# A two-part state-space kernel: one small load moved between DMA queues, two products moved to VectorE, half-block stores at the end, and a new hand-written order

## The chip, the cores and the metric

The kernel runs on one core of a Trainium2 chip. A core has five engines with a queue each: TensorE (PE in the profile, its weight loads PEld), VectorE (DVE), ScalarE (ACT), GpSimd (POOL) and SyncE (SP), and 16 DMA engines that carry the transfers which SP and ACT issue. The metric is the device time of one execution in microseconds, the median of several runs. Lower is better.

## What is computed

Two independent sequence operators over 2048 steps and 640 channels, their outputs laid side by side in one (1, 2048, 1280) bfloat16 result.

```python
# A: a diagonal complex recurrence between two dense products
Lam_bar = jnp.exp(jnp.exp(log_dt) * Lam)
B_bar = ((Lam_bar - 1.0) / Lam)[:, None] * (B_re + 1j * B_im)
Bu = jnp.einsum("bld,pd->blp", x + 0j, B_bar)
for t in range(L):
    h = Lam_bar[None, :] * h + Bu[:, t, :]
y = 2.0 * jnp.einsum("blp,dp->bld", hseq, Cmat).real + x * Dskip
# B: a 4-tap filter on k, a product with v, a long convolution by FFT, a gate
k_shift = sum of four shifted copies of k, each times a tap of shift_k
kv = k_shift * v
y = irfft(rfft(kv) * rfft(ssm_k))[:S] + kv * ssm_D
out_b = q * y
```

## The kernel before

**Part A.** The 2048 steps are split into four phases q (step modulo 4), the 640 states into five blocks j of 128. `z{q}{j}` is the input product of phase q and block j on PE, ten matmuls of 128x512 (two parts, real and imaginary, by five pieces of the contraction), evicted by ACT to the tile F (`ze{q}{j}`, line 764). The phases are made in the order 1, 2, 3, 0, and each has to have the previous phase's sum, turned by the state's eigenvalue, added to it. That addition is either four more matmuls with the diagonal matrices diagL (lines 437 and 438) or, for the pairs (q, j) in the set `BYDVE`, five DVE operations after the eviction (`zd{q}{j}`, `dve_odd`, lines 464 to 468). Before, `BYDVE` holds (2, 0), (2, 1) and (2, 2). Then a scan over phase 0 runs on DVE (`rs{j}`, line 453), `h0{j}` turns it back, `h1{j}` to `h3{j}` spread it to the other phases (`dve_odd` again), and `p{i}{q}` on PE multiplies a block of 128 rows of phase q by the output matrix (20 matmuls of 128x320, line 478). Three quarters of the later blocks get x times Dskip added on DVE while they leave PSUM (`yo{i}{q}`, line 508, from `xd{i}`, line 504); the rest get it by three small matmuls per half (line 485) and leave by ACT (line 489). `yd{i}{q}` stores them.

**Part B.** It goes over five groups G of 128 channels: transposing loads of k and v (`kT`, `vT`), a copy of k with its two halves of partitions swapped (`kS`), the four taps as 32 small matmuls in two halves (`tap{G}_{m}`, line 553), the product with v on DVE straight from PSUM (`kv{G}_{m}`, line 558), a store of it to memory (`kvo`) and a reload in another layout (`kvs`). The long convolution is a transform in two steps on PE (`s1h`, `s2h` for the filter, `s1k`, `s2k` for kv, lines 576 and 590 to 593), a complex product on DVE in two halves (`y{G}_{hf}`, lines 603 to 606), the way back (`inv`, lines 614 to 617), a transposing DMA (`zt`), a last small product (`fin`, line 635), the gate with q on DVE (`ob`, line 640) and a store (`od`). For each group, ACT makes all evictions between these steps (`s1he`, `s2he`, `s1ke`, `s2ke`, `zs`). The set `KVA` names groups whose taps ACT evicts into the tile kT (`kve`), so that DVE multiplies once over the whole group in SBUF; before, it is empty.

**The start.** Small rows (log_dt, the two Lambda rows, Dskip, the taps) are loaded on ACT's queue. SP loads B, block by block (B0, B1, then x1 in two pieces, then B2 to B4, x2 and so on). PE runs eight matmuls on zeros (`wm0`, `wm1`), transposes the small rows (`vt`) and the blocks of B (`bt0` to `bt7`, line 389), whose evictions go to ACT (line 395) and DVE (line 397). From the small rows come, through exp, rho, rr, Fi, trig1, lam on ACT and DVE, the eigenvalue and its powers (`pow`, on POOL). `G0` to `G3` are sine and cosine tables for the transforms (ACT, lines 373, 153, 154); POOL prepares their phases (`gp`) and those of the scan's tables (`tp`). `dcol` loads a column of ssm_D in two strided DMAs (line 515, on ACT's queue), which `had{G}` (line 537) adds to the filter.

**What sets the order.** There is no loop left in the program text that orders the work: every step is an item of a plan (`make_plan`) with an engine, an assumed cost and its dependencies, and `ORDER` is a written list of all of them, with the PSUM slot behind an `@`. Each engine and each DMA queue gets its items in that order and works through them without overtaking. A PSUM slot is free again when the item that evicts it is done. DMAs use a fixed number of completion slots in turn, so an issue can also wait for an older DMA of the same slot. The costs in the plan serve only the search that made the list.

## Time and profile before

| | us |
|---|---|
| median of 3 runs | 202.76 (202.07 to 203.42) |
| the profiled execution | 203.54 |
| its span, first to last instruction | 201.8 |
| PE busy | 191.2 |
| DVE busy | 169.2 |
| ACT busy | 146.6 |
| POOL busy | 31.4 |

The profile of one execution gives a page (busy time, the span in 40 slices, groups of instructions by line) and a trace that can be asked for timelines and for busy time by stretch. In a timeline the columns are start, duration (of the merged run), engine, line, operation, output and inputs, count, and in brackets how long the engine sat idle before it and what ended that. PEclk or "granted clock" is the share of full TensorE speed that was granted. A group's line ends with its busy total, the mean duration of one in ns, and the idle time just before.

### The profile page before, as it was taken

To read this page: it belongs to the slowest core of one execution; us is meant where nothing else is said; L and a number is where in the kernel's file an instruction comes from. 1 tells how busy PE (TensorE), PEld (TensorE's weight loads), DVE (VectorE), ACT (ScalarE), POOL (GpSimd) and SP (SyncE) were. 2 spreads that over 40 slices of the span, in tenths; PEclk is the share of its full clock that TensorE was granted. 3 is DMA by queue.
4 is the path that set the end of the run, shared out by engine and by line. 5 is a ranking of instruction groups with operands and counts; after the bars stand their busy time and mean duration, and the time that the engine had idled before them with its cause. 6 is when DMAs were issued, how large, how long until landed. Compare 5 with 4: busy or idle time off the path is not lost.

```text
span 201.8 us, 5456 instructions
## 1 busy us (share of the span) xinstructions
PE 191.2 (95%) x2294; PEld 135.1 (67%) x2303; DVE 169.2 (84%) x279; ACT 146.6 (73%) x178; POOL 31.4 (16%) x68
## 2 busy tenths in 40 slices
PE   7848999999999999999999999999999999899992
PEld 2525444444444875488878897689977998787771
DVE  2822578999989999999999999999999999985561
ACT  2268769979985987899978899689977799350010
POOL 7881898900000000000000000000000000000000
PEclk9995899999999999999999999999999999999999
DMA  5999999749968999998999899799839569739944
GB/s 142 223 235 204 181 202 233 127 132 227 195 127 236 198 158 257 178 190 131 169 241 207 180 190 184 182 258 184 178 97 142 143 137 187 131 79 192 209 145 131
DMA packets 110667, 36.01 MB, mean 178 GB/s; under 512 B 104877, under 2 KB 109618, under 8 KB 110642
## 3 DMA queue, kind: packets, MB, share of 16 engines
q1 hardware_dynamic: 110544, 35.64, 91.7%
q8 instruction: 18, 0.29, 0.7%
q14 instruction: 7, 0.06, 0.1%
q10 hardware_dynamic: 98, 0.02, 0.1%
HBM read 10.66 MB, written 7.86 MB: 92 GB/s over the span
## 4 chain that ended last, share of the span: by engine, by line
PE 89%; DMA 3%; POOL 3%; ACT 2%; issue 1%; DVE 1%; ACTq 0%; DVEq 0%; POOLq 0%
PE ps L478 20%; PE ps L434 20%; PE ps L576 6%; PE ps L553 5%; PE ps L590 5%; PE ps L592 4%; PE ps L591 4%; PE ps L593 4%; DMA zz<-zz 3%; PE ps L438 3%; PE ps L635 3%; PE ps L437 2%; PE ps L614 2%; PE ps L616 2%; PE ps L615 2%; PE ps L617 2%
## 5 line engine op out<-in xcount | busy, mean ns | idle before, releaser
L434 PE MATMUL ps<-xT,BT 128*128 128x512 bf16 x187 | 47.3, 390 | 0.6 <-issue 0.4
L478 PE MATMUL ps<-Cs,F 128*128 128x320 bf16 x320 | 46.9, 300 | 0.0
L478 PEld LDWEIGHTS <-F 128*128 128x128 bf16 x320 | 29.9, 98 | 11.0
L434 PEld LDWEIGHTS <-BT 128*128 128x128 bf16 x192 | 18.6, 100 | 23.0 <-issue 3.1
L580 ACT CAST As_h<-ps 128x1024 bf16<-128x1024 f32 x20 | 20.3, 1022 | 7.9 <-PE ps L576 7.9
L764 ACT CAST F<-ps 128x1024 bf16<-128x1024 f32 x20 | 20.1, 1007 | 5.1 <-PE ps L434 3.2
L622 ACT CAST zz<-ps 128x1024 bf16<-128x1024 f32 x20 | 19.2, 1039 | 5.7 <-PE ps L617 5.5
L580 ACT CAST As_kv<-ps 128x1024 bf16<-128x1024 f32 x20 | 20.0, 1035 | 2.7 <-PE ps L576 2.7
L596 ACT CAST Xs<-ps 128x1024 bf16<-128x1024 f32 x20 | 19.9, 1052 | 0.6 <-PE ps L593 0.6
L596 ACT CAST Hf<-ps 128x1024 bf16<-128x1024 f32 x20 | 19.8, 1072 | 0.5 <-PE ps L593 0.5
L590 PE MATMUL ps<-As_kv,Gre 128*128 128x128 bf16 x80 | 17.6, 220 | 0.0
L590 PE MATMUL ps<-As_h,Gre 128*128 128x128 bf16 x80 | 17.6, 220 | 0.0
L614 PE MATMUL ps<-Xs,Hre 128*128 128x128 bf16 x80 | 17.6, 220 | 0.0
L592 PE MATMUL ps<-As_h,Gim 128*128 128x128 bf16 x80 | 17.6, 220 | 0.0
L592 PE MATMUL ps<-As_kv,Gim 128*128 128x128 bf16 x80 | 17.6, 220 | 0.0
L616 PE MATMUL ps<-Xs,Him 128*128 128x128 bf16 x80 | 17.6, 219 | 0.0
L591 PE MATMUL ps<-As_h,nGim 128*128 128x128 bf16 x80 | 17.5, 219 | 0.0
L615 PE MATMUL ps<-Xs,nHim 128*128 128x128 bf16 x80 | 17.5, 219 | 0.0
L593 PE MATMUL ps<-As_h,Gre 128*128 128x128 bf16 x80 | 17.5, 219 | 0.0
L591 PE MATMUL ps<-As_kv,nGim 128*128 128x128 bf16 x80 | 17.5, 219 | 0.0
L593 PE MATMUL ps<-As_kv,Gre 128*128 128x128 bf16 x80 | 17.5, 219 | 0.0
L617 PE MATMUL ps<-Xs,Hre 128*128 128x128 bf16 x80 | 17.5, 219 | 0.0
(163 smaller groups left out, 454.7 us busy)
## 6 DMA issues: line engine op xcount, KB each, us to landing
h_st<-in_B_ssm_k_dram SPq DMA_DIRECT2D x10, 256.0 KB, 4.7
kv_rows<-vT SPq DMA_DIRECT2D x5, 512.0 KB, 5.1
kv_st<-kv_rows SPq DMA_DIRECT2D x10, 256.0 KB, 4.1
qb<-in_B_q_dram SPq DMA_DIRECT2D x5, 512.0 KB, 4.8
out_dram<-yo SPq DMA_DIRECT2D x16, 160.0 KB, 3.6
out_dram<-qb SPq DMA_DIRECT2D x5, 512.0 KB, 6.5
kS<-kT SPq DMA_DIRECT2D x10, 129.0 KB, 2.5
BT<-in_A_x_dram SPq DMA_DIRECT2D x3, 320.0 KB, 5.2
```

The source lines that it names most:

```text
L434: mm(ps[:, r, :], lhsT=self.BT[:, r, k, j * 128:(j + 1) * 128], rhs=xT[:, k, :], start=(k == 0), stop=(prev is None and k == NT - 1))
L478: mm(ps[:, b, 0:320], lhsT=self.F(p, j)[:, r, ts], rhs=self.Cs[:, r, j, c0:c0 + 320], start=(j == 0 and r == 0), stop=((i, p // 2) in SKD ...
L580: self.nc.scalar.copy(out=As[:].rearrange("p k (h s) -> p h k s", h=2)[:, :, :, 16 * q:16 * q + 16], in_=ps[:].rearrange("p h (k s) -> p h ...
L590: mm(o_re, lhsT=self.Gre[:, k1, :], rhs=re, start=True, stop=False)
L591: mm(o_re, lhsT=self.nGim[:, k1, :], rhs=im, start=False, stop=True)
L592: mm(o_im, lhsT=self.Gim[:, k1, :], rhs=re, start=True, stop=False)
L593: mm(o_im, lhsT=self.Gre[:, k1, :], rhs=im, start=False, stop=True)
L596: self.nc.scalar.copy(out=dst[:, :, o:o + 128 * n], in_=ps[:] if n == 4 else ps.rearrange("p (r n) -> p r n", r=2))
L614: mm(o_re, lhsT=self.Hre[:, k1, :], rhs=yre, start=True, stop=False)
L615: mm(o_re, lhsT=self.nHim[:, k1, :], rhs=yim, start=False, stop=True)
L616: mm(o_im, lhsT=self.Him[:, k1, :], rhs=yre, start=True, stop=False)
L617: mm(o_im, lhsT=self.Hre[:, k1, :], rhs=yim, start=False, stop=True)
```

## The change

- The load of the ssm_D column (`dcol`) is issued on SP's queue, after x2, instead of on ACT's.
- `BYDVE` also holds (2, 3) and (2, 4): phase 2 of all five blocks gets its sum on DVE instead of by matmuls.
- `KVA` holds groups 1 and 2: ACT evicts their taps, DVE multiplies once in SBUF. The next load of kT then waits for that product.
- The last output block, (3, 3), is made, added to and stored in two halves of 320 columns.
- Some assumed costs in the plan are other (pow 6.0 instead of 4.2, gam 3.4 instead of 2.4, the latency of the B loads), some ACT steps are bound behind the loads on ACT's queue, and `ORDER` is a new list throughout, with other PSUM slots.
- `act_ha` and `dve_ha` are new functions that nothing calls, since the set `HA` is empty.

```diff
-BYDVE = {(2, j) for j in range(3)}
-KVA = set()
+BYDVE = {(2, j) for j in range(5)}
+KVA = {1, 2}
...
+HA = set()
+LAST = {(3, 3)}
...
-    def pe_proj(self, i, p, ps):
+    def pe_proj(self, i, p, ps, bs=(0, 1)):
         mm = self.nc.tensor.matmul
+        self.part["p", i, p] = ps
...
-        for b in range(2):
+        for b in bs:
...
+    def dve_yoh(self, y, i, q, b):
+        c = slice(320 * b, 320 * b + 320)
+        self.nc.vector.tensor_tensor(out=self.__dict__[f"yo{y}"][:, q % 2, c], in0=self.part["p", i, q][:, b, 0:320],
+                                     in1=self.xd[:, i % 2, q % 2, c], op=ALU.add)
+
+    def store_yoh(self, y, i, q, b):
+        c = slice(320 * b, 320 * b + 320)
+        self.nc.sync.dma_start(out=self.o2[512 * i:512 * i + 512, c].rearrange("(m p) d -> p m d", p=4)[q],
+                               in_=self.__dict__[f"yo{y}"][:, q % 2, c])
...
-            self.nc.scalar.dma_start(out=self.dcol_b[64 * h:64 * h + 64:16, :, 0:61], in_=src)
+            self.nc.sync.dma_start(out=self.dcol_b[64 * h:64 * h + 64:16, :, 0:61], in_=src)
...
-    dma("dcol", "ACT", 1.0, 0.0, ["~l_sk", "pc"], lambda: K.load_dcol(), lat=2.4)
+    dma("dcol", "SP", 1.1, 0.3, ["~x2", "pc"], lambda: K.load_dcol())
...
-    A("exp", "ACT", 0.3, ["vc"], lambda: K.act_exp())
+    A("exp", "ACT", 0.3, ["vc", "~l_sk"], lambda: K.act_exp())
...
+            if (i, q) in LAST and sk:
+                hd = [f"h{q}{j}" for j in range(NT)] + cs_all
+                A(f"p{i}{q}a", "PE", 10 * P320, hd, lambda ps, i=i, q=q: K.pe_proj(i, q, ps, (0,)), take=f"p{i}{q}", group=f"P{x}")
+                A(f"yo{i}{q}a", "DVE", 0.42, [f"p{i}{q}a", f"xd{i}"] + old, lambda y=y, q=q, i=i: K.dve_yoh(y % 2, i, q, 0), group=f"P{x}")
+                dma(f"yd{i}{q}a", "SP", 0.45, 0.4, [f"yo{i}{q}a"], lambda y=y, i=i, q=q: K.store_yoh(y % 2, i, q, 0), group=f"P{x}")
...
```

The first steps of both lists, engine by engine (items in the order in which the engine gets them):

```
ACT before: l_ldt l_lim l_lre l_dsk l_sk exp btf0 bte1 dcol rr G3 ze10 bte3 bte4 ze11 trig1 tab0 ze12 aRM bte5 ze13 ze21 ze20 G2
ACT after:  l_ldt l_lim l_lre l_dsk l_sk btf0 exp rr bte1 G2 trig1 bte3 ze10 ze11 bte4 tab0 ze12 bte5 G3 ze21 aRM ze20 ze22 tab1
PE before:  wm0 wm1 vt bt0 bt2 bt1 skt z10a z11a z10 bt3 z11 bt6 bt4 bt5 z12 bt7 z13 z21 z20 z14 z22 tap0_0 tap0_1 z30
PE after:   wm0 bt0 vt wm1 bt1 skt bt2 z10a z10 bt3 z11a bt6 z11 bt4 bt5 z12 z21 bt7 z20 z22 z13 tap0_1 tap0_0 z24 z23 z31 z14 z30 z01
DVE before: dc zer vc dc2 bte0 bte2 rho Fi skc bte6 rden bte7 dS0 lam dD dRM dL zd20 zd21 kv0_0 dS1 zd22 kv0_1 cs0 cs1 had0 rs0
DVE after:  dc vc bte0 rho Fi bte2 skc zer dc2 bte6 rden dD lam dL bte7 dS0 zd21 dRM zd20 kv0_1 dS1 zd22 kv0_0 cs1 nG cs0 zd23 cs3 cs2 had0 zd24 rs1
SP before:  B0 B1 x1a x1 B2 B3 B4 x2 kT0 vT0 x3 kS0 CT0 x0 CT1 hs0 kvo0 kT1 vT1
SP after:   B0 B1 x1a x1 B2 B3 B4 x2 dcol kT0 x3 kS0 vT0 CT0 CT1 kT1 x0 kS1 hs0 kvo0
```

The last steps of the new list on PE are inv4 (four parts), p12, p13, p22, fin4_1, p23, the first half of p33, fin4_0, p32, the second half of p33; on SP the last are the stores of the first half of (3, 3), of (2, 3), of group 4's output (od_4), of (3, 2) and of the second half of (3, 3).

## The prediction

> **What bounds the kernel now.** I read the page's busy table and its 40 slices, then busy time by stretch, then the timelines of the first 25 us and of the end, then the groups by line.

> ```profile
> PE 191.2 (95%) x2294; PEld 135.1 (67%) x2303; DVE 169.2 (84%) x279; ACT 146.6 (73%) x178; POOL 31.4 (16%) x68
> ...
> DVE  2822578999989999999999999999999999985561
> ...
> PEclk9995899999999999999999999999999999999999
> ```
> ```profile
> 15.90:21.90 6.00, 5.76 (x29) 3.48 (x30) 1.13 (x4) 4.34 (x8) 1.37 (x2) 0.51 1.14 174
> ...
> 57.60:100.00 42.40, 42.14 (x579) 28.96 (x576) 40.57 (x59) 35.93 (x40) 0.00 (x0) 1.00 1.03 182
> 100.00:140.00 40.00, 40.00 (x637) 33.31 (x632) 38.73 (x64) 34.04 (x40) 0.00 (x0) 1.00 1.03 205
> ```
> Columns: stretch, length, busy us of PE, weight loads, DVE, ACT, POOL, granted clock, DMA share, GB/s. PE never stops between 16 us and 170, and DVE is busy 96 to 97% from 30 on. So two engines bound the middle together. What PE alone saves there, DVE takes back. The exception is the start:

> ```profile
> 10.29 1.22 ACTq L515 DMA_DIRECT2D dcol_b<-in_B_ssm_D_dram  x2
> 11.56 0.21 ACT L273 ACTIVATE rr<-rho 128x5 f32<-128x5 f32 x1 [4.78 <-DVE Fi L267]
> 11.77 1.28 ACT L373 ACT_TABLE_LOAD   x1
> ...
> 14.88 0.99 ACT L764 CAST F<-ps 128x1024 bf16<-128x1024 f32 x1
> ```
> ```profile
> 15.92 2.29 PE L389 MATMUL ps<-ident,zz 128*128 128x128 bf16 x20 [3.52 <-ACT F L764]
> 18.00 2.76 PE L434 MATMUL ps<-xT,BT 128*128 128x512 bf16 x6
> ...
> 22.16 10.09 PE L434 MATMUL ps<-xT,BT 128*128 128x512 bf16 x45
> ```
> ACT ends its evictions at 6.78 and then sits until 10.29: the next entry of its queue is dcol's load, whose first half waits for a slot that B2's load holds. rr, a table load, G3 and the first z eviction (ze10) stand behind it. PE needs that bank and idles 3.52 us. The granted clock then reads 0.50 from about 15.0 to 21.8, so matmuls come every 0.43 us instead of 0.21 until 21.8: (21.8 - 15.9)/2 = 2.95 us more. The gap costs PE 6.5 us.

> [...]

> **The change, part by part**, against the profiled execution (203.54 us: span 201.8 and 1.74 around it; the median of the runs, 202.76, is 0.78 below it).

> *dcol to SP.* ACT's queue loses the wait and 1.22 us of issue; vc now also precedes bte0, and Fi precedes bte2 on DVE. Working through the new order with durations of before: warm-up ends 3.33 (five at 0.43); B0, issued 0.73 to 1.60, lands about 4.0 to 4.5 (its kind takes 3.3); bt0, vt; btf0 ends 5.6 on ACT, exp 5.85; DVE's dtf starts 6.3 where it started at 7.88, so rho ends 7.5 and Fi 9.8; rr 7.7, bte1 8.3, table load and G2 (3.1) 11.45, trig1 12.0, bte3 12.9, ze10 13.8. On PE: z10 waits for x1 (between 8.3 and 9.2; it was no later than 9.2 before), bt3 for B2 (10.3, when dcol could start), z11a for bte2 (11.0), then bt6, z11, bt4 and bt5 run to 14.4. Before, PE stood at that point of its work (less 1.1 us for bt6, bt4, bt5) at 15.92, and cold. So PE's 3.52 shrinks to about 1.1 in small pieces and the half clock goes: 2.4 + 2.95 = 5.4 gained.

> What SP pays: 1.22 us between x2 and kT0, so x2 ends 13.2, dcol 14.4, kT0 16.3, x3 19.9, kS0 21.3, vT0 24.6, CT0 28.5, CT1 32.1, kT1 34.0, x0 37.1 (issue times of before's rows). had0, the reader of dcol, ran at 45.5: covered by 30 us.

> *Two more block sums on DVE (z23, z24).* PE loses 8 matmuls of 0.216: 1.73. DVE gains two sets of five operations; an undisturbed set starts every 2.25 us (164.01 to 166.26): +4.5.

> *KVA for groups 1 and 2.* ACT gains 4 evictions of 1.02: 4.1 us, where it had 6.5 us idle of 42.4 (57.6 to 100): covered on average, not at each bank. DVE loses 4 products from PSUM at 1.22 alone, 1.17 in pairs (4.7) and gains two over 128x2048 in SBUF, 1.23 each (2.5). The next kT load now waits for that product instead of the tap matmuls; kT2 and kT3 stand on SP ahead of kvs, hs loads that PE wants some 10 us later by the order.

> ```profile
> L468 DVE TENSOR_TENSOR F<-F,rot 128x1024 bf16<-128x1024 bf16 x18 | 13.2, 734 | 0.6
> ...
> L604 DVE TENSOR_TENSOR Xs<-Xs,Hf 128x2048 bf16<-128x2048 bf16 x10 | 12.3, 1226 | 0.6
> ...
> L558 DVE TENSOR_TENSOR vT<-ps,vT 128x1024 bf16<-128x1024 f32 x10 | 12.0, 1218 | 1.9 <-PE ps L553 1.6 <-issue 0.2
> ```
> So DVE has 4.5 - 4.7 + 2.5 = 2.3 us more work.

> *Where DVE starts.* Its long chain begins with cs, which started at 42.08. Ahead of that DVE lost time: zd22 took 36.06 to 40.95, 4.9 instead of 2.25, while POOL ran tp4 and gp0. In the new order dL ends about 16.8; zd21 waits for ze21 (21.2), kv0_1 for vT0 (28.2: issue 21.3 and the 6.9 that vT takes), then dS1, zd22, kv0_0 to 33.4, and cs1 waits for CT1: issue 28.5 and CT0's kind of 6.5 gives 35.0. So DVE leads by 7.1, less 2.3 of work: 4.8. Its last y block ended at 176.4; the two orders do the same other work up to there, so it ends at 171.6 if DVE idles as before (4.7 us from 42 to 176). The order is another: bounds for its idle are 0 and double. At the first y block (about 69) PE, ACT and DVE arrive within 1 us of each other by the rows; for this I add one wait of the size of before's longest in the middle, 0.9: 172.5.

> [...]

> *Last block in halves.*
> ```profile
> 198.22 0.82 DVE L508 TENSOR_TENSOR yo<-ps,tabs 128x640 bf16<-128x640 f32 x1 [1.95 <-PE ps L478]
> ...
> 194.85 0.38 SPq L656 DMA_DIRECT2D out_dram<-qb  x1
> 196.30 3.10 SPq L493 DMA_DIRECT2D out_dram<-yo  x2
> ```
> The last addition halves from 0.82 to between 0.41 and 0.82; an extra issue (0.4) lies under PE. But od_4 landed about 194.85 + 6.5 = 201.35, nearly last too. In the new order, after the last y block come inv4 (3.6), p12, p13, p22 (8.2), fin4_1, p23, p33a (4.6), fin4_0 (0.5), then ob4_0 (1.2) and od_4 (6.9), with the drains 24.8; before it was 25.4. Gain 0.6; bounds 0 and 1.

> Sum: 172.5 + 24.8 = 197.3 of span, 4.5 less. 202.76 - 4.5 = **198.3**.

> **Rivals.** (1) PE alone sets the end: 5.4 + 1.7 + 0.6 = 7.7 less, 195.1. For it: DVE's idle could fall, and PE's lead at 49 us by the rows is 6.5. Against: DVE at 97%. Chance 0.11.

> (2) The clock starts late. Before, eight warm-up matmuls ran on without a break to 4.78 and the next transposes came at the full rate. Now PE pauses from 3.3 to about 4.0, and a stretch with 0.93 us of wait (15.0 to 18.4) did not raise the clock. If it stays at 0.5 until 21.8, as it was before, PE's 5 us of work between 8.3 and 14.4 take 10 instead of the 6.1 they have there (3.9 late), and the 3.5 us left to 21.8 do 1.7 us less: 5.6 lost. PE's bound of rival 1 (194.1 of span) + 5.6 + the wait of 0.9 is 200.6 of span, 201.6: no measurable change. Against: at half rate PE is busy without a break from 4.5 to 8.2. [...] Chance 0.14.

> (3) Slower: a new gap later. Place: z01, about 40 us, which needs x0; x0 now stands behind kT1 on SP, and kT1 waits for both tap matmuls; ze31 must also have freed the bank. By the rows x0 lands 34.0 + 5.4 to 6.6, at 39.4 to 40.6, and PE arrives at 39.7. A gap of 3.5 costs itself and, as in before, 3 us at half clock; 6.5 against the 4.5 gained gives 204.8, so from a gap of 3.5 on it is slower; at 4.2, 205.5. For it: four engines and SP are packed anew and ACT has 4 us more. Against: PE had no such gap after 16 us before. Chance 0.18.

> (4) Halves do nothing since od_4 ends last: 0.6 of the sum, inside the forecast's range.

> **The numbers.** Forecast 0.57, its own range 196.3 to 200.3. About 1% (2 us) is what a measurement of this kernel can tell. Faster: 0.57 + 0.11 = 0.68; within 1%: 0.14; slower: 0.18. The range reaches from PE's bound, 195.0, to 203.5, past rival 2, and leaves out rival 3 (0.18).

> **What would show it.** Right: no ACT wait ahead of rr, ze10 near 13.8, PE without a 3 us gap, granted clock 1.00 in slices 4 and 5, cs starting near 35, the last y block ending near 172, DVE about 2 us busier. Wrong: 0.50 anywhere after 5 us, a PE wait over 2.5 us at z01 or at the taps, DVE idle above 8 us between cs and the last y block.

## The result and the profile after

The changed kernel takes 195.62 us (195.00 to 197.87, 4 runs) where the kernel before took 202.44 (202.07 to 203.42, 4 runs): a ratio of 0.9676 [0.9591, 0.9761]. Measured once more on another chip (run c_after) it takes 196.56 us (195.6 to 198.41, 6 runs), a ratio of 0.9757 [0.9711, 0.9804] to the kernel before on that chip. So the change is worth 4.9 to 6.6 us by the two ratios; 4.5 were forecast. The sign is right, and the gain was put too low: 196.56 lies inside the forecast's own range (196.3 to 200.3), while 195.62 lies below it, 0.5 above rival 1's 195.1, and only inside the whole range (195.0 to 203.5).

The profiled execution took 195.0 us, its span 193.2. That of the kernel before (203.54, mean granted clock 0.983) is one of its longest, so the 8.6 us between the two spans are more than the change is worth. From the page of the changed kernel, the busy line and the same two rows of slices as in the prediction:

```profile
PE 187.7 (97%) x2295; PEld 133.4 (69%) x2295; DVE 173.3 (90%) x288; ACT 150.2 (78%) x182; POOL 36.9 (19%) x68
...
DVE  1988999999999999999999999999999899985852
...
PEclk9999999999999999999999999999999999999999
```

DVE is at 80% or more from the second slice to the thirty-sixth, where before it stood at 20 to 70% in the third to sixth, and the clock has no weak slice: the 0.50 stretch is gone. ACT at the start:

```profile
6.21 0.21 ACT L275 ACTIVATE rr<-rho 128x5 f32<-128x5 f32 x1 [0.94 <-DVE rho L257]
6.91 1.28 ACT L375 ACT_TABLE_LOAD   x1
...
11.86 1.02 ACT L795 CAST F<-ps 128x1024 bf16<-128x1024 f32 x1
```

No wait ahead of rr beyond 0.94 us for its own input, and ze10 (the last line) runs at 11.86 instead of 14.88. PE and the queue of SP over the same stretch:

```profile
13.13 1.06 PE L391 MATMUL ps<-ident,zz 128*128 128x128 bf16 x16
14.02 4.48 PE L436 MATMUL ps<-xT,BT 128*128 128x512 bf16 x20
```
```profile
27.12 3.73 SPq L771 DMA_TRANSPOSE Cs<-in_A_C_im_dram  x1
31.02 2.06 SPq L551 DMA_TRANSPOSE kT<-in_B_k_dram  x1
33.12 3.84 SPq L414 DMA_TRANSPOSE xT<-in_A_x_dram  x1
```

PE finishes bt4 and bt5 by about 14.2, without the 3.52 us gap, and its matmuls come every 0.22 us. CT1 (the first SP line) is issued at 27.12, and DVE's long chain follows its landing:

```profile
33.40 0.89 DVE L350 SCALAR_TENSOR_TENSOR Cs<-Cs,gam,Xs 128x640 bf16<-128x640 bf16 x1 [0.15 <-DMA Cs<-in_A_C_im_dram]
...
168.31 1.29 DVE L637 TENSOR_TENSOR Xs<-Xs,rot 128x1024 bf16<-128x1024 bf16 x2
```

So cs starts at 33.4 (42.08 before) and the last y block ends at 169.6 (176.5 before): 6.9 of the 8.6 us between the two spans. The other 1.7 lie behind it, in the tail of 23.6 us:

```profile
187.64 0.38 SPq L687 DMA_DIRECT2D out_dram<-qb  x1
188.89 0.82 DVE L529 TENSOR_TENSOR yo<-ps,tabs 128x640 bf16<-128x640 f32 x1 [1.49 <-PE ps L499]
...
190.25 0.49 DVE L534 TENSOR_TENSOR yo<-ps,tabs 128x320 bf16<-128x320 f32 x1 [0.54 <-PE ps L499]
190.77 0.33 SPq L539 DMA_DIRECT2D out_dram<-yo  x1
```

The stretch from cs to the last y block, first in the kernel before, then in the changed one (length, then PE, weight loads, DVE, ACT, POOL busy, clock, DMA share, GB/s):

```profile
42.08:176.42 134.34, 133.26 (x1864) 100.69 (x1868) 129.68 (x200) 113.89 (x129) 0.00 (x0) 1.00 0.96 182
```
```profile
33.40:169.52 136.12, 135.62 (x1883) 102.26 (x1882) 131.84 (x207) 118.46 (x134) 8.47 (x15) 1.00 0.96 185
```

The stretch became 1.8 longer and starts 8.7 earlier. DVE has 2.2 us more work in it and idles 4.3 instead of 4.7; PE idles 0.5 of 136. Both are nearly full there; which of them sets the end, the third group of runs shows.

### The profile page after: what moved, and what is told of

Read it like the earlier page. It is cut to its first block, busy times and chain, and to the rows that moved or that the text cites. A ratio compares the mean times of both kernels' runs of the same rounds, so it can differ in the third digit from the quotient of the medians.

```text
span 193.2 us, 5445 instructions
## 1 busy us (share of the span) xinstructions
PE 187.7 (97%) x2295; PEld 133.4 (69%) x2295; DVE 173.3 (90%) x288; ACT 150.2 (78%) x182; POOL 36.9 (19%) x68
## 4 chain that ended last, share of the span: by engine, by line
PE 83%; DMA 9%; ACT 2%; SPq 2%; DVE 1%; issue 1%; ACTq 0%; DVEq 0%
PE ps L499 22%; PE ps L436 19%; DMA xT<-in_A_x_dram 6%; PE ps L607 5%; PE ps L621 5%; PE ps L623 5%; PE ps L624 5%; PE ps L622 5%; PE ps L584 3%; PE ps L666 3%; DMA zz<-zz 3%; PE ps L645 2%; PE ps L440 2%; PE ps L439 2%; PE ps L648 2%; PE ps L647 2%
## 5 line engine op out<-in xcount | busy, mean ns | idle before, releaser
L436 PE MATMUL ps<-xT,BT 128*128 128x512 bf16 x192 | 45.3, 379 | 0.8 <-DMA xT<-in_A_x_dram 0.6
L436 PEld LDWEIGHTS <-BT 128*128 128x128 bf16 x192 | 18.1, 98 | 22.2 <-issue 1.3
```

The source lines that it names most:

```text
L436: mm(ps[:, r, :], lhsT=self.BT[:, r, k, j * 128:(j + 1) * 128], rhs=xT[:, k, :], start=(k == 0), stop=(prev is None and k == NT - 1))
```

## The experiments

My theory (A): dcol's wait on ACT's queue was the loss, mostly through where DVE's long chain starts; from there DVE sets the end. Rivals: (B) PE alone sets the end, by its gap and the half clock; (C) the gain is in the two sums moved, in the taps or in the halves, and dcol matters little. The runs of one group below shared a chip and the runs of the kernel before on it.

### First group: dcol, the clock, PE's slack

**e1_dcol_sp**, the kernel before with dcol alone moved:

```diff
-            self.nc.scalar.dma_start(out=self.dcol_b[64 * h:64 * h + 64:16, :, 0:61], in_=src)
+            self.nc.sync.dma_start(out=self.dcol_b[64 * h:64 * h + 64:16, :, 0:61], in_=src)
...
-pp bt1@6 ... z10a@2 dcol gp2 B4 ... x2 G3 z10
+pp bt1@6 ... z10a@2 gp2 B4 ... x2 dcol G3 z10
```

> The kernel before, with one change: dcol is issued on SP after x2; its place in the list moves with it. Theory A (the start gives most of the gain: the load on ScalarE's queue delays the first z eviction, PE idles and its clock halves): rr starts about 9.1 instead of 11.56, ze10 about 12.4, PE's gap shrinks from 3.52 to about 1, the granted clock stays 1.00, and the time falls by 3.5 to 5.5 us, to 197 to 199. Theory B (the new order and the moved work in the middle give most): the time falls by less than 2.5 us, since the middle is as full as before.

Measured: 198.69 us (198.58 to 198.77) against 202.22; ratio 0.9843 [0.9765, 0.9921]. ACT waits 1.46 us before rr, PE's gap shrinks to 0.70, the clock is 1.00, cs starts at 37.69 (4.4 earlier) and the last y block ends at 171.5 (5.0 earlier). One DMA issue on another queue brings 3.2 us [1.6, 4.8], by the ratio, of the 4.9 to 6.6.

**e2_after_dcol_act**, the changed kernel with dcol back on ACT's queue, between bte1 and the table load:

```diff
-            self.nc.sync.dma_start(out=self.dcol_b[64 * h:64 * h + 64:16, :, 0:61], in_=src)
+            self.nc.scalar.dma_start(out=self.dcol_b[64 * h:64 * h + 64:16, :, 0:61], in_=src)
...
-den rho skt@4 B2 Fi rr bt2@2 bte1@0 gp1 ...
+den rho skt@4 B2 Fi rr bt2@2 bte1@0 dcol gp1 ...
```

> The changed kernel, with one change undone: dcol is issued on ScalarE's queue again, between bte1 and the first sine table. Theory A: ScalarE waits again for a slot that an older load holds (to about 10 to 11) and issues for 1.2 us, so ze10 comes 3 to 4 us later, PE stands still for about 3 us and may lose its clock: 3 to 6 us slower than the changed kernel (199 to 201.5). Theory B: less than 2 us slower.

Measured: 200.17 (197.81 to 201.41), ratio 0.9914 [0.9867, 0.9961], apart from both intervals of the changed kernel. ACT and PE in its trace:

```profile
10.08 1.21 ACTq L546 DMA_DIRECT2D dcol_b<-in_B_ssm_D_dram  x2
11.32 1.28 ACT L375 ACT_TABLE_LOAD   x1 [4.42 <-DMA dcol_b<-in_B_ssm_D_dram]
```
```profile
16.00 1.93 PE L391 MATMUL ps<-ident,zz 128*128 128x128 bf16 x16 [2.69 <-ACT BT L397]
```

ACT's last eviction ended at 6.9, yet the issue begins only at 10.08, as at 10.29 in the kernel before, although the list around it is another. In the trace of the kernel before, dcol's line waits on ACT's queue, ahead of its first half, for the semaphore on which the first of B2's two loads reports its landing: that load, issued at 6.49, reports for the last time at 10.21, 3.72 us later, and the issue begins at 10.29. All 111 DMAs there carry one of eight such semaphores, the completion slots, in turn, and dcol's two halves have the same two as B2's loads. In e2 the issue begins 3.83 us after that of B2's load (6.25), in e3 3.24 after it (6.23); that it is the same wait there is inferred from these times. PE's gap is back (2.69), the clock falls again, cs starts at 36.64. This is the old fault, put back.

**e3_before_fill**, the kernel before with 14 matmuls on zeros in PE's gap; nothing reads them:

```diff
-WM = (5, 3)
+WM = (5, 3, 14)
...
-... bt3@6 ze10@2 z11 skc@4 bte3@6 ...
+... bt3@6 ze10@2 z11 skc@4 wm2@4 wme2@4 bte3@6 ...
```

> The kernel before, with 14 matmuls on zeros (about 3 us) added on PE in the gap ahead of bt6, into a bank that is free there; nothing waits for them. They keep PE busy while it waits for the first z eviction, and do not shorten the wait. Theory A splits the 6.5 us of PE into 3.5 of wait and 2.95 of half clock: here the clock stays at 1.00 after 15 us and the time falls by 2 to 3 us. If the half clock was hidden (the engines it delays had time in hand): within 1 us of before.

Measured: 200.38 (199.84 to 200.53), ratio 0.9918 [0.9889, 0.9947]: 1.7 us [1.1, 2.2] by the ratio. ACT still waits 3.59 before rr (4.78 in the profile of the kernel before). The fill and what follows it on PE:

```profile
12.59 3.19 PE L141 MATMUL ps<-diagL 128*128 128x512 bf16 x14
15.62 1.28 PE L389 MATMUL ps<-ident,zz 128*128 128x128 bf16 x20
```

The transposes take 1.28 us for 20 where they took 2.29, and the clock stays at 1.00. The 1.7 us are not to be set against the 2.95 of the prediction, since those belong to one execution. The record has the mean granted clock of 53 executions of the kernel before, on the chips of the three groups:

| mean granted clock | executions | us, median (range) |
|---|---|---|
| 0.983 | 8 | 203.2 (202.85 to 203.65) |
| 0.989 to 0.992 | 36 | 202.0 (201.21 to 202.67) |
| 0.998 to 1.000 | 9 | 200.4 (199.97 to 200.67) |

The profiled execution is of the first row: 6.8 us at 0.50. A mean of 0.991 over 200 us is an estimated 3.6 us at 0.50 (2 x 0.009 x 200), half as long; the same sum gives 6.9 for the profiled one. The others left no trace, so that their half rate also falls behind dcol's wait is inferred from the equal steps. By this reading the program loses the clock for about 6.8 us, for half of that or not at all, and pays about 2.8, 1.6 or 0 us at the end, nearly all that PE loses. e3 stands at 200.4, where the executions of the last row stand, and its 1.7 is what the half clock costs a typical execution. The rest of e1's gain, from 200.4 to 198.7, comes with the shorter wait.

In e3, cs starts at 37.75, as early as in e1 (37.69), but the last y block ends at 173.5 and not at 171.5. Two things still lie behind there: PE, which starts the transposes at 15.62 instead of 13.48, and DVE, whose first two operations of cs take 1.6 us each instead of 0.9 while POOL still works. So where cs starts does not by itself tell where the stretch ends, and these runs do not divide the 1.9 us between PE and DVE.

**e4_after_pe_more**, the changed kernel with ten matmuls more (the first of each part of phase 3 is made twice, 2.2 us of PE):

```diff
         for r in range(2):
+            if p == 3:
+                mm(ps[:, r, :], lhsT=self.BT[:, r, 0, j * 128:(j + 1) * 128], rhs=xT[:, 0, :], start=True, stop=True)
             for k in range(k0, NT):
```

> The changed kernel with 10 matmuls more on PE (2.16 us): the first matmul of each half of z30 to z34 is made twice, with no other change. If VectorE sets the end, as the forecast had it: at most 0.7 us slower. If PE alone sets the end (rival 1): 2.2 us slower. If both are bound together: 1 to 2 us.

Measured: 199.29 (198.36 to 200.94), ratio 0.9883 [0.9796, 0.997]. That is above the changed kernel's 0.9676 and 0.9757, but its interval touches that of the second [0.9711, 0.9804], and the changed kernel was not on this chip. It decides nothing alone; e9 repeats it larger, with the control beside it.

### Second group: each of the other parts undone

There was no control of the changed kernel on this chip, so only intervals that lie apart from both of its own count. An order that was searched for other parts may also pay for the undoing, so a loss here is an upper bound of the part's worth.

**e5_after_dve_more** (the first operation of each phase 3 sum twice, 2.0 us of DVE):

```diff
+        if p == 3:
+            v.tensor_scalar_mul(out=self.rot_p, in0=h, scalar1=l[0])
         v.tensor_scalar_mul(out=self.rot_p, in0=h, scalar1=l[0])
```

> The changed kernel with 2.0 us more on VectorE: the first of the five operations of h31 to h34 and h30 is made twice (0.40 us of pitch each). If VectorE sets the end, as the forecast had it: 2 us slower. If PE alone sets the end (rival 1): at most 0.7 us slower. If both are bound together: 1 to 2 us.

Measured: 197.85 (197.27 to 198.98), ratio 0.9789 [0.9739, 0.9839]. Not told apart from the changed kernel; too small a dose.

**e6_after_whole_last** (the last block in one piece):

```diff
-LAST = {(3, 3)}
+LAST = set()
...
-... yd12 p33a@6 yo23@4 fin4_0@4 yo33a p32@2 ob4_0@4 yd33a yd23 od_4 p33 yo32@2 yd32 yo33@6 yd33
+... yd12 yo23@4 fin4_0@4 p32@2 ob4_0@4 yd23 od_4 p33@6 yo32@2 yd32 yo33@6 yd33
```

> The changed kernel with the last block (3, 3) made, added to and stored in one piece, after p32. Forecast's step: the halves are worth 0.6 us, bounds 0 and 1. If od_4 ends last either way: 0.

Measured: 198.21 (197.69 to 200.31), ratio 0.982 [0.9754, 0.9885], which overlaps. The traces say more than the times: the stretch from the last y block's end to the end of the span is 25.25 us here, as in the kernel before (25.3), e1 (25.5) and e3 (25.1), and 23.6 to 24.2 in all the ten traces with halves. The end of e6, its last two PE steps and its last addition:

```profile
186.27 0.63 PE L666 MATMUL ps<-Mq,zz 128*128 128x64 bf16 x16 [0.91 <-DVE yo L529]
...
192.37 0.82 DVE L529 TENSOR_TENSOR yo<-ps,tabs 128x640 bf16<-128x640 f32 x1 [1.89 <-PE ps L499]
```

The halves are worth 1.1 to 1.6: 0.33 for the shorter last addition (0.82 to 0.49), and 0.91 because the first half's ten matmuls stand where fin4_0 would wait for its PSUM slot until the addition of (2, 3) is done.

**e7_after_z23_pe** (the sum of (2, 3) back on PE):

```diff
-BYDVE = {(2, j) for j in range(5)}
+BYDVE = {(2, j) for j in (0, 1, 2, 4)}
...
-... z30@4 hs0 ze14@2 zd23
+... z30@4 hs0 ze14@2
```

> The changed kernel with the sum of z23 back on PE (four matmuls more, 0.86 us; VectorE 2.25 us less). If VectorE sets the end: about 2 us faster. If PE alone does: 0.9 us slower. If both are bound together: within 0.7 us.

Measured: 198.79 (197.75 to 199.03), ratio 0.9819 [0.9773, 0.9865]. It takes 2.25 us from DVE and gives PE 0.86. If DVE alone set the end it would be up to 2 us faster than the changed kernel; nothing of that is seen. Whether it is slower is not resolved.

**e8_after_kva1** (the taps of group 2 again multiplied straight from PSUM):

```diff
-KVA = {1, 2}
+KVA = {1}
...
-... kve2_0@2 z04@6 y0_1 s1ke1_3@0 kve2_1@4 ... z02@2 kv2_0 s1ke1_1@4 ...
+... kv2_0@2 z04@6 y0_1 s1ke1_3@0 kv2_1@4 ... z02@2 s1ke1_1@4 ...
```

> The changed kernel with group 2's taps multiplied on VectorE straight from PSUM again, two operations in the place of the two evictions on ScalarE (ScalarE 2 us less, VectorE 1.1 us more and earlier). If VectorE sets the end: 1 to 2 us slower. If PE alone does and its banks come free in time: within 0.7 us.

Measured: 200.64 (198.98 to 204.13), ratio 0.9907 [0.987, 0.9945], apart from both: by the ratios 3.0 us above c_after and 4.7 above the first measurement. PE's longest wait and the product before it, from PE's and from DVE's timeline:

```profile
79.51 0.62 PE L607 MATMUL ps<-R,kv_st 64*128 64x128 bf16 x16 [2.79 <-DVE vT L589]
```
```profile
78.24 1.22 DVE L589 TENSOR_TENSOR vT<-ps,vT 128x1024 bf16<-128x1024 f32 x1
```

DVE reaches the second product at 78.24, and until it ends (79.46) its PSUM slot is not free for the next step on PE. This one wait of 2.79 is the most of the loss; DVE's extra work, by the rows 1.1 us per group, is the small part. It is what this order pays without the eviction, not what the part brought: the kernel before has no such evictions, and its PE idles only 1.1 us in the whole stretch from cs to the last y block.

### Third group, with the control beside it: which engine sets the end

**c_after** is the changed kernel itself.

> The changed kernel itself, unchanged, on the chip of the three runs beside it, since the runs with one part undone stood 2 to 5 us above its first measurement and it was not on their chip. If the chip makes no difference: a ratio to before of 0.968. If transfers land later on such a chip (x2 held PE for 0.8 to 1.1 us there): about 0.975.

Its times are told above; its profiled execution was the longest of its six (198.41, span 196.5). There the last y block ends 2.8 us later than in the first profile, at 172.4, and two PE waits that the first profile doesn't have are 2.75 together; the second stands behind an eviction of ACT that waited for a transposing DMA still reading its tile. PE, then ACT:

```profile
17.25 2.33 PE L436 MATMUL ps<-xT,BT 128*128 128x512 bf16 x10 [1.23 <-DMA xT<-in_A_x_dram]
...
130.83 0.62 PE L607 MATMUL ps<-R,h_st 64*128 64x128 bf16 x16 [1.52 <-ACT zz L653]
```
```profile
129.76 2.84 ACT L653 CAST zz<-ps 128x1024 bf16<-128x1024 f32 x3 [3.12 <-DMA zz<-zz]
```

So one and the same order loses 0 or some 3 us by when DMAs land.

**e9_after_pe_more2** (phases 0 and 3: 20 matmuls more, 4.3 us of PE) and **e10_after_dve_more2** (all three multiplications of each phase 3 sum twice, 4.6 us of DVE by the rows):

```diff
+            if p in (0, 3):
+                mm(ps[:, r, :], lhsT=self.BT[:, r, 0, j * 128:(j + 1) * 128], rhs=xT[:, 0, :], start=True, stop=True)
```
```diff
+        for _ in range(2 if p == 3 else 1):
+            v.tensor_scalar_mul(out=self.rot_p, in0=h, scalar1=l[0])
+            v.tensor_scalar_mul(out=self.rot_x[:, 0, :], in0=h[:, 1, :], scalar1=l[2])
+            v.tensor_scalar_mul(out=self.rot_x[:, 1, :], in0=h[:, 0, :], scalar1=l[1])
```

> The changed kernel with 20 matmuls more on PE (4.3 us): the first matmul of each half of z30 to z34 and z00 to z04 is made twice. Against the changed kernel on the same chip. If VectorE sets the end: at most 1.5 us slower. If PE alone sets it: 4.3 us. If the two are bound together: 2 to 4 us, and the same sort of share for the run with more work on VectorE.

> The changed kernel with 4.6 us more on VectorE: the first three of the five operations of each h3 are made twice (0.92 us of pitch, five times). Against the changed kernel on the same chip. If VectorE sets the end: 4.6 us slower. If PE alone sets it: at most 1.5 us. If the two are bound together: 2 to 4 us.

Measured: e9 201.02 (200.18 to 202.88), ratio 0.998 [0.9944, 1.0017]; e10 200.08 (199.15 to 200.6), ratio 0.9922 [0.9892, 0.9951]. Against the control's 196.56, 4.3 us of PE cost 4.5, and 4.6 us of DVE cost 3.5, both good to about 1.1 us by the intervals. The same stretch, cs to the last y block, in c_after, e9 and e10:

```profile
33.36:172.43 139.07, 136.63 (x1885) 103.27 (x1890) 132.32 (x208) 119.52 (x135) 7.71 (x17) 1.00 0.96 182
```
```profile
33.24:175.20 141.96, 140.37 (x1900) 104.65 (x1905) 132.53 (x208) 119.84 (x135) 8.62 (x17) 1.00 0.95 178
```
```profile
34.14:174.34 140.20, 136.15 (x1877) 102.40 (x1882) 136.62 (x223) 119.28 (x135) 7.15 (x15) 1.00 0.93 180
```

Length less busy time: with more PE work PE idles 1.6 and DVE 9.4; with more DVE work PE idles 4.1 and DVE 3.6. In c_after it is 2.4 and 6.8, in the changed kernel's first profile 0.5 and 4.3. With more DVE work PE waits for DVE, as it does in neither profile of the changed kernel nor in e9: 1.44 for the PSUM slot of a gate product and 1.8 in three pieces for complex products (e5, with less than half the dose, has 0.64 and 0.83 at these places). The two longest:

```profile
139.91 0.63 PE L667 MATMUL ps<-Mq,zz 128*128 128x64 bf16 x16 [1.44 <-DVE qb L672]
...
150.70 0.23 PE L646 MATMUL ps<-Xs,Hre 128*128 128x128 bf16 x1 [1.26 <-DVE Xs L638]
```

So work added to either engine moves the end. With DVE alone at the end e9 was expected at most 1.5 slower, with PE alone e10 at most 1.5; both cost more. Neither A nor B is right alone.

In the same stretch of the changed kernel's first profile weight loads fill 102.26 of 136.12 us (75%) and PE is busy for 99.6%. 4.3 us more of PE cost 4.5, so the quarter that the weight loads leave free was no headroom.

**e11_x2_earlier** (x2 issued ahead of B4, what it delays moved behind z21, dcol behind hs0), a try at a version better than both:

```diff
-... bte2@2 B4 z10 x2 trig1 ... bte6@4 dcol bt4@0 ze11@2 bt5@6 rden ... z21@0 dL ... pp bte5@6 bt7@4 ... ze21@0 z22@4 ... hs0 ze14@2 ...
+... bte2@2 x2 B4 z10 trig1 ... bte6@4 bt4@0 ze11@2 rden ... z21@0 bt5@6 dL ... pp bt7@4 ... ze21@0 bte5@6 z22@4 ... hs0 dcol ze14@2 ...
```

> The changed kernel with three items moved: x2 is issued ahead of B4 on SP (bt5 and its eviction follow z21 and ze21), and dcol behind the first h load instead of behind x2. If the wait for x2 at z21 and the 1.3 us that dcol takes on SP ahead of kT0, vT0 and the two C loads still stand on the path: 0.8 to 1.5 us faster than the changed kernel. If they are hidden: within 0.5 us.

Measured: 196.47 (196.13 to 197.67), ratio 0.9753 [0.9715, 0.9792]: the same as the control. The wait of 1.23 for x2 is gone, but PE waits 0.60 for x0 at 40.07 instead. The 0.6 us that are left of it are less than the two intervals can tell (about 0.8 each), so the run leaves open what x2's landing is worth.

## Why the prediction was right, and where not

*The bound at the start* (dcol's wait, the gap, the clock): right in kind. e1 and e2 show it from both sides, one undone in the old kernel, one put back in the new.

*PE's 5.4 gained*: against the profiled execution it came, and a little more (bt5 done at 14.2 instead of 14.4, ze10 at 12.9 instead of 13.8, rr at 6.4 instead of 7.7). The base was mis-sized: 2.95 us of half clock are those of the profiled execution, and most executions of the kernel before lose about half of that (1.7 by e3), yet the whole was taken off the median.

*DVE starts at 35.0*: mis-sized by 1.6. It was 33.4, and 33.0 to 34.2 in every trace with this start but e2's. In the first profile, e7 and e10 the last thing that DVE waits for is CT1's landing, as forecast, 6.3 us from issue to use in the first against 6.5; in c_after, e5, e6 and e9 it is ACT's copy from the first C load, with 0.45 to 0.67 of wait, so two things arrive there nearly together. The step that failed is SP's queue: I put CT1's issue at 28.5, it was 27.12, since vT0 and CT0 took 2.26 and 3.46 of SP's time instead of the 3.3 and 3.9 of before's rows.

*DVE's 2.3 more work*: measured 2.2. *DVE idles 4.7 as before, and 0.9 for one more wait*: 4.3 and no such wait in the first profile, 6.8 in the control's. The 0.9 lies between them. In the control the wait is PE's, at another place than the first y block.

*The tail of 24.8*: 23.6 in the first profile, 24.1 in the control's. The chain that I followed, through od_4, is not the one that ends last: od_4, issued at 187.6, landed in 4.0 us, where I had 6.9, and the second half of (3, 3), stored from 190.77 on, came last. (My terms add up to 25.0, not 24.8.) That the length comes near is luck. Gain of the halves 0.6, bounds 0 and 1: mis-sized, beyond my upper bound. I counted the shorter addition alone and not that the first half covers fin4_0's wait for a PSUM slot (0.91 in e6). Rival 4 is out: od_4 landed more than 1 us before the end at 193.2.

*The sum*: in the first profile the last y block came 2.9 us earlier than the 172.5 forecast (1.6 from cs, 1.3 from waits) and the tail was 1.2 shorter. In the control's the last y block came at 172.4, the forecast, but by errors that cancel: the start 1.6 earlier, DVE's waits 1.2 and its work 0.3 longer. That the control's time is inside the forecast's own range is luck to that extent.

*DVE sets the end, PE has 3 us to spare* (the distance between forecast and rival 1): this step failed. e9 costs all of its 4.3 us, e7 gains nothing from a DVE relieved of 2.25. The room that I gave PE isn't there. Rival 1 (195.1, PE alone) is nearer to the first measurement, but it fails too, as e10 costs 3.5: PE and DVE end together.

*KVA costed by DVE's work* (4.7 less, 2.5 more): the count is right and missed what the part does for PE in the new order. There, without it for group 2, e8 loses 3.0 or more, mostly by a PSUM slot that DVE frees late.

*Rival 2* (the clock starts late) did not come: full rate by about 6 us (transposes come every 0.06 us from 5.87, every 0.11 from 3.29), three warm-up matmuls at 4.75 still at 0.43 us each (the clock column reads 1.00 there all the same). *Rival 3* (a gap at z01): x0 did come last there, and PE waited 0.18 us, until 39.74; the place was right and the price next to nothing, since x0 was issued at 33.1 and not at 34.0.

Open: how the 1.7 to 3.4 us beyond e1 divide between the taps, the two sums, the halves and the new order. The halves' 1.1 to 1.6 are measured in the traces. Against c_after the undone parts add up to more than the 4.9 that there is (e2 3.2, e8 3.0, the halves 1.2), so they overlap or pay for the undoing, and the runs do not split them.

## What to carry to other kernels

A load issued on a compute engine's queue can hold that engine until an older transfer ends, longer than its own issue time (here ACT stood still for 3.51 us, 6.78 to 10.29, ahead of 1.22 us of issue): look for an engine idle ahead of a DMA issue, and move that load to a queue with nothing urgent behind it. Where two engines are both nearly full in a stretch (here PE 99.6% and DVE 96.9%), price a change by what it does to each, and don't give either of them slack before a run with work added to that engine has shown it. Count for a split or for an early eviction also which PSUM slot comes free sooner and who waits for it: with the part undone that wait was longer (0.91, 2.79) than the work saved (0.33, 1.1). And look at the granted clock of several executions before one of them becomes the base of a sum.

## What the runs showed of the hardware

```profile
14.00:16.00 2.00, 0.00 (x1) 0.00 (x1) 1.49 (x5) 1.97 (x6) 1.92 (x3) 0.92 0.94 191
16.00:18.00 2.00, 2.00 (x17) 1.81 (x17) 2.00 (x3) 2.00 (x3) 1.92 (x2) 0.50 1.21 257
18.00:20.00 2.00, 2.00 (x8) 0.83 (x7) 0.29 (x1) 1.74 (x3) 1.77 (x6) 0.73 1.20 184
20.00:22.00 2.00, 2.00 (x11) 0.89 (x10) 0.00 (x0) 1.25 (x2) 1.84 (x5) 1.00 0.86 198
```

If the rate only steps between 0.5 and 1, as it does in the profiled execution of the kernel before (1.00 up to 14.98, 0.50 to 21.81, 1.00 from there), 0.92 over the first stretch puts the fall at about 15.7 and 0.73 over the third the rise at about 19.1: an estimated 3.4 us at half rate. The 6.83 us of the kernel before are two such lengths, with PE idle until 15.92 in the first. Why one program pays for none, one or two of them is not shown. Matmuls on zeros in the gap (e3) kept the clock at 1.00 from 12.59 to 24.3.

The same kernel spread over 195.0 to 198.4 us in its ten runs; the two profiled executions of it differ by two waits behind DMAs, 1.23 and 1.52 us. The first, for x2, stands in six of the nine traces with this start (0.57 to 1.23), so the first profile, which lacks it, is not the common case. Why those DMAs land later in some is not settled.
